# Three hand-written instruction orders of a retention and soft-MoE attention kernel are replaced

## The chip, the core and the metric

The kernel runs on one core of one Trainium2 chip. The metric is the device time of one execution in microseconds (us), less is better; the time of a version is the median of its runs. The engines of a core are TensorE (PE in the profile, with its weight loads as PEld), VectorE (DVE), ScalarE (ACT), GpSimd (POOL) and SyncE (SP, which issues the transfers here).

## What is computed

Eight batches of 576 tokens pass through two layers. The first is retention with eight heads of 64, the second a mixture of four attention experts of which each token takes the two best.

```python
scores = scale * np.matmul(q, k.transpose(0, 1, 3, 2))     # per head
ret = scores * Dmat            # gamma_h ** (i - j) for i >= j, else 0
x = np.matmul(ret, v)          # heads side by side: B x 576 x 512
logits = x @ w_gate            # the two best of four experts, softmax over them
for e in range(E):
    q, k, v = x @ wq[e], x @ wk[e], x @ wv[e]
    a = softmax(causal(scale * (q @ k.transpose(0, 2, 1))))
    ye = a @ v @ wo[e]
    out += weight_of_e * ye
```

## The kernel before, in words

The tokens are cut into 36 tiles of 128 rows (two chunks of 64; in four tiles the chunks come from two batches), and three tiles make a group, so there are 12 groups. Work runs as a pipeline over groups: in step j the retention of the tiles 3j+1 to 3j+3 is made, group j-1 gets its value, key and query projections and its gate, group j-2 its expert attention, and group j-3 its output projection. One unit of expert attention is one tile of one group, except that each third group ends in two half units ("tails"), so that three kinds of steps repeat. With t the number of earlier 128-blocks that a unit looks back on, a step works on units of t = 0, 1, 2 (kind A, j = 2, 5, 8, 11), t = 3, 0, 1 (kind B, j = 3, 6, 9) or t = 2, 3 and two tails of t = 4 (kind C, j = 4, 7, 10).

The order of all instructions on PE, DVE, ACT and POOL is written out by hand in three lists of tokens: `HEAD` (fills the pipeline), `STEP` (played for j = 2 to 11) and `TAIL` (drains it). `play` walks a list and calls one helper for each token; each engine then runs its instructions in that order and waits in that order. SP is not in the set `ORDERED`, so the order of its transfers is not given by the lists.

The tokens that matter here, with the line of the helper's instruction:

- Retention, argument is the tile: `qm` scores (PE, L197), `qa` their copy (ACT, L204), `qp` the causal cut (POOL, L210); `tm`/`tv` state products (PE, L170) and sums (DVE, L183, L185); `om`/`oa` product with the old state (PE, L223) and copy (ACT, L232); `wm`/`wv` product within the chunk (PE, L243) and sum (DVE, L252, L253); `dc` decay of the loaded values (POOL, or DVE with `:v`, L157); `sc` scaling (L261, L263), `xh`/`xl` the rounded part (ACT, L275) and the rest (L280).
- Projections: `vm` values and gate logits (PE, L335), `va` (ACT, L344, L349) and `vv` (DVE, L357, L358) their copies; `km`/`ka`, `hm`/`ha` keys and queries (PE, L316; ACT, L323, L325); `g.0` to `g.4` the gate (DVE, part 1 on ACT, L370 to L391). `wh`/`wl` split a weight into a rounded part and a rest (ACT, L298; DVE, L303), `tb` makes a decay table (ACT, L150).
- Units, first digit the unit, second the expert or block group: `s` scores (PE, L419; tails L427), `r` row limits (DVE, L443; tails L446), `e` powers (ACT, L456), `n` the factors (DVE, L464 to L466), `ma`/`mv` the scaling of one expert's powers on ACT (L480) or DVE (L482), `tt` transposes of up to four blocks into one bank (PE, L498), `ca`/`cv` their copy on ACT (L509) or DVE (L511), `ym` product with the values (PE, L532 to L539), `ya`, `yp`, `yl` its copy and split (ACT, POOL; DVE in the end).
- `pm`/`pa` output projection (PE, L565) and its copy with the store (ACT, L570).

All products land in PSUM, in one pool of eight banks. A product takes the bank that, by the plan made when the kernel is built, has come free first, and waits until that bank's last reader is done. Banks are requested where the products stand in the lists, so the lists also set which copy frees whose bank. A scores token of t = 0 or 1 takes two banks, one of t = 2, 3 or a tail four, `qm`, `om`, `wm`, `tm` two, the others one.

```python
pool = ctx.enter_context(tc.tile_pool(name="ps", bufs=8, space=bass.MemoryType.PSUM))
ctx.enter_context(tc.manual_schedule(engines=ORDERED))
```

Of the kernel before, what the change touches and what calls it, by code (L numbers as in the profile page):

```python
# [66 lines left out]
TAIL = """
@12 s.0 r.00 r.01 r.02 r.03 km.0 ka.0 e.00 e.01 e.02 e.03 n.0 ma.00 mv.01 ma.02 mv.03 hm.0 ha.0 s.1 r.10 r.11 r.12
r.13 km.1 ka.1 e.10 e.11 e.12 e.13 n.1 ma.10 mv.11 ma.12 mv.13 hm.1 ha.1 s.2 r.20 r.21 r.22 r.23 vm.0 va.0 vv.0 e.20
e.21 e.22 e.23 n.2 ma.20 mv.21 ma.22 mv.23 vm.1 va.1 vv.1 vm.2 va.2 vv.2 @13 s.0 r.00 r.01 r.02 r.03 @12 g.0 g.1 g.2  # L70
g.3 g.4 pm.0 pa.0 pm.1 pa.1 tt.00 cv.00 tt.01 ca.01 tt.02 cv.02 tt.03 ca.03 tt.10 ca.10 tt.11 cv.11 tt.12 ca.12
tt.13 cv.13 tt.20 cv.20 tt.21 ca.21 tt.22 cv.22 tt.23 ca.23 @13 s.1 r.10 r.11 r.12 r.13 e.00 e.01 e.02 e.03 n.0
ma.00 mv.01 ma.02 mv.03 @12 pm.2 pa.2 pm.3 pa.3 ym.0 ya.0 yp.0 ym.1 ya.1 yp.1 ym.2 ya.2 yp.2 @13 tt.00 cv.00 tt.01
ca.01 tt.02 cv.02 tt.03 ca.03 e.10 e.11 e.12 e.13 n.1 ma.10 mv.11 ma.12 mv.13 s.2 r.20 r.21 r.22 r.23 s.3 r.30 r.31
r.32 r.33 e.20 e.21 e.22 e.23 n.2 ma.20 mv.21 ma.22 mv.23 pm.0 pa.0 pm.1 pa.1 e.30 e.31 e.32 e.33 n.3 ma.30 mv.31
ma.32 mv.33 pm.2 pa.2 pm.3 pa.3 tt.10 ca.10 tt.11 cv.11 tt.12 ca.12 tt.13 cv.13 tt.20 cv.20 tt.21 ca.21 tt.22 cv.22
tt.23 ca.23 tt.30 ca.30 tt.31 cv.31 tt.32 ca.32 tt.33 cv.33 ym.0 yl.0 ym.1 yl.1 ym.2 yl.2 ym.3 yl.3 @14 pm.0 pa.0
pm.1 pa.1 pm.2 pa.2 pm.3 pa.3
"""


# [606 lines left out]
```

## Time and profile before

| | us |
|---|---|
| median of 3 runs | 471.57 (471.18 to 471.76) |
| the profiled execution | 473.03 |
| its span, first to last instruction | 470.9 |
| PE busy | 439.0 (93%) |
| ACT busy | 284.9 (61%) |
| DVE busy | 275.6 (59%) |
| POOL busy | 202.9 (43%) |

The profiled execution is 2.1 us longer than its span and 1.5 us above the median. The profile was read in this order: busy shares of the engines, busy time by stage, what PE waited for, the timeline of every engine around those waits, the chain of work that ended last, and the granted clock of TensorE in each stage.

### The profile page before, as it was taken

How to read it: one execution, taken by the hardware profiler on the slowest of the kernel's cores; microseconds unless marked ns; L12 is line 12 of the kernel's file. 1: busy time of each engine (PE TensorE's matmuls, PEld its weight loads, DVE VectorE, ACT ScalarE, POOL GpSimd, SP SyncE). 2: the span in 40 equal slices, each digit the busy share in tenths (PEclk: the TensorE clock that was granted, in tenths of full speed). 3: DMA queues.
4: the chain of work that ended last, by engine and by line, in shares of the span. 5: the costliest groups of instructions: out<-in, count | busy, mean ns of one | idle time of the engine just before them, and what ended most of it. 6: DMA issues, size and time to landing. Idle time of an engine off the chain costs nothing.

```text
span 470.9 us, 18834 instructions
## 1 busy us (share of the span) xinstructions
PE 439.0 (93%) x7916; PEld 397.5 (84%) x7916; DVE 275.6 (59%) x1083; ACT 284.9 (61%) x830; POOL 202.9 (43%) x260
## 2 busy tenths in 40 slices
...
PEclk9679878999999999999999999999999999999989
...
GB/s 273 407 118 100 221 124 101 56 162 125 84 135 124 1 145 197 21 151 169 53 165 125 1 128 212 7 151 185 41 173 84 1 22 51 3 1 35 35 68 68
DMA packets 18899, 50.90 MB, mean 108 GB/s; under 512 B 2304, under 2 KB 9088, under 8 KB 18816
## 3 DMA queue, kind: packets, MB, share of 16 engines
...
q8 instruction: 63, 1.03, 0.9%
q14 instruction: 20, 0.16, 0.1%
...
## 4 chain that ended last, share of the span: by engine, by line
PE 76%; ACT 9%; DVE 8%; issue 4%; DMA 1%; POOL 1%; SPq 0%; ACTq 0%; DVEq 0%; POOLq 0%
PE pj L316 22%; PE pv L335 11%; PE pt L498 7%; PE ss L419 6%; PE ys L532 6%; PE po L565 5%; PE own L243 5%; PE st L170 4%; PE qk L197 3%; PE old L223 3%; ACT p L456 2%; PE ys L539 2%; ACT p L480 2%; DVE sm L464 2%; PE ys L536 2%
## 5 line engine op out<-in xcount | busy, mean ns | idle before, releaser
L456 ACT ACTIVATE p<-p,nm 128x128 f32<-128x128 f32 (+8 forms) x144 | 79.8, 562 | 7.7 <-DVE nm L443 6.8
L280 POOL TENSOR_TENSOR xl<-x,xh 128x512 fp32r<-128x512 f32 x32 | 40.9, 1278 | 97.0 <-ACT xh L275 97.0
L443 DVE CUSTOM_DVE_ANT_0 p<-ss,mask 128x128 f32<-128x128 f32 (+7 forms) x128 | 51.0, 454 | 35.5 <-PE ss L419 35.5
L210 POOL TENSOR_SCALAR_AFFINE_SELECT p<-p 64x512 f32<-64x512 f32 x72 | 49.2, 683 | 33.1 <-ACT p L204 30.3
L480 ACT ACTIVATE p<-p,sm 128x64 f32<-128x64 f32 (+4 forms) x72 | 37.0, 556 | 38.5 <-DVE sm L466 38.5
L511 DVE COPY pth<-pt 128x512 f32<-128x512 f32 (+2 forms) x56 | 33.0, 612 | 43.6 <-PE pt L498 42.9
L555 POOL CAST yh<-y 128x256 fp32r<-128x256 f32 (+1 forms) x36 | 13.7, 382 | 80.9 <-ACT y L543 80.9
L419 PE MATMUL ss<-k,q 64*64 64x512 f32 (+7 forms) x512 | 42.2, 414 | 3.5 <-ACT ot L570 3.5
L263 POOL TENSOR_TENSOR x<-x,gi 128x512 f32<-128x512 f32 x26 | 33.6, 1290 | 21.8 <-DVE x L253 19.6
L498 PE MATMUL pt<-con,p 128*128 128x128 f32 x360 | 41.7, 273 | 0.5 <-ACT ot L570 0.5
L498 PEld LDWEIGHTS pt<-con,p 128*128 128x128 f32 x360 | 40.0, 141 | 1.2 <-ACT ot L570 0.7
L532 PE MATMUL ys<-pth,vn 128*64 128x128 f32 (+1 forms) x640 | 39.2, 254 | 0.0
L243 PEld LDWEIGHTS own<-p,vk 64*64 64x64 f32 x1152 | 28.1, 144 | 10.8 <-issue 8.9
L464 DVE TENSOR_SCALAR sm<-sm 128x4 f32<-128x4 f32 (+1 forms) x40 | 14.4, 361 | 34.8 <-ACT p L456 34.3
L157 POOL TENSOR_TENSOR vk<-vk,con 128x512 f32<-128x512 f32 x33 | 34.5, 1045 | 0.3
L243 PE MATMUL own<-p,vk 64*64 64x64 f32 x1152 | 30.9, 230 | 2.9 <-issue 2.6
L170 PE MATMUL st<-vk 64*64 64x64 f32 x1024 | 25.1, 230 | 8.3 <-issue 6.3
L204 ACT ACTIVATE p<-qk 128x256 f32<-128x256 f32 x72 | 23.5, 381 | 13.3 <-PE qk L197 12.8
L509 ACT ACTIVATE pth<-pt 128x512 f32<-128x512 f32 (+2 forms) x48 | 24.7, 548 | 10.1 <-PE pt L498 10.1
L532 PEld LDWEIGHTS ys<-pth,vn 128*64 128x64 f32 x640 | 29.0, 138 | 1.4 <-issue 0.9
L482 DVE TENSOR_SCALAR p<-p,sm 128x64 f32<-128x64 f32 (+4 forms) x104 | 29.1, 333 | 1.4
L253 DVE TENSOR_TENSOR x<-x,own 128x256 f32<-128x256 f32 (+1 forms) x72 | 25.5, 386 | 7.5 <-ACT x L232 6.6
...
## 6 DMA issues: line engine op xcount, KB each, us to landing
...
rg<-wraw SPq DMA_DIRECT2D x1, 8.0 KB, 7.9
```

The lines of the kernel that those rows point to most:

```text
L170: mm(ps[r][HALF[g], s, u], vk[HALF[r], s, 1, h], vk[HALF[r], s, 0, h], start=True, stop=True)
L210: gp.affine_select(w, w, pattern=[[0, 8], [1, 64]], base=0, channel_multiplier=-1, compare_op=OP.is_ge, fill=0.0)
L243: mm(ps[r][HALF[u], g, i], vk[HALF[r], s, 0, 2 * g + u], p[HALF[r], g, s, u], start=True, stop=True)
L280: e.tensor_sub(xl, x32, f(xh))
L316: mm(ps, ww[:, kc, p * 128:(p + 1) * 128], xx[:, kc], start=(i == 0), stop=(i == 11))
L335: mm(ps, xx[:, kc, l0:l0 + 128], ww[:, kc], start=(i == 0), stop=(i == 11))
L419: mm(ps[e][HALF[p]], q[p][HALF[z], l0 + 64 * s:l0 + 64 * s + 64], k[p][HALF[z], kb:kb + ws[e]], start=True, stop=True)
L443: v.tensor_tensor_reduce(p32[:, e, :ws[e]], ps[e], mask[:, 576 - ws[e]:], -1.0, BIG, OP.add, OP.min, nm[:, e:e + 1])
L456: act(p32[:, e, :ws[e]], p32[:, e, :ws[e]], AF.Exp, bias=nm[:, b:b + 1], scale=-1.0, accum_out=sm[:, 0, e:e + 1])
L480: act(o, i, AF.Copy, scale=rs[:, e:e + 1])
L498: nc.tensor.transpose(pt[:, z], src, ident)
L532: mm(py[HALF[z], p], VN[n0 + j][:, e * D:(e + 1) * D], src, start=(j == 0), stop=False)
```

## The change

Only the three lists are rewritten; no helper, tile or buffer is touched. Each list holds as many tokens as before. In `STEP` the order on PE stays mostly as it was up to `km.0`, with these moves: `om.0` comes before `qm.1`, `s.1` before `om.1`, `pm.3` before `pm.2`, and the transposes of the first units stand between `hm.0`, `hm.1` and `km.1` instead of behind all four. On ACT the copies `va`, `pa`, `qa`, `oa` stand ahead of scalings; on DVE `n.0` stands ahead of `vv.0`; on POOL `dc.2` opens the step, and `dc.3` stands ahead of `qp.2`. Of each step's scalings two go from ACT to DVE net, and of its transposed blocks' copies one more is on DVE. In `HEAD` three multiplies and subtractions move to DVE and three to POOL (`dc.1`, `sc.4`, `sc.5` to POOL; `dc.6`, `dc.7`, `xl.1` to DVE), the weight splits move forward or back in their queues, and `hm.0` goes behind `vm.2`. In `TAIL` the units of the last two groups, which alternated in blocks, are mixed token by token.

```diff
 STEP = """
-qm.1 qa.1 qp.1 om.0 oa.0 s.0 r.00 r.01 r.02 r.03 wm.0 wv.0 tm.1 tv.1 lx.3 lk.4 sc.0 dc.2 e.00 e.01 e.02 vm.0 va.0
-vv.0 e.03 n.0 ma.00 mv.01 ma.02 mv.03 xh.0 xl.0 vm.1 va.1 vv.1 pm.0 pa.0 pm.1 pa.1 qm.2 qa.2 qp.2 om.1 oa.1 s.1 r.10
-r.11 r.12 r.13 wm.1 wv.1 tm.2 tv.2 lx.4 lk.5 sc.1 dc.3 e.10 e.11 e.12 vm.2 va.2 vv.2 e.13 n.1 ma.10 mv.11 ma.12
-mv.13 xh.1 xl.1 pm.2 pa.2 pm.3 pa.3 qm.3 qa.3 qp.3 om.2 oa.2 s.2 r.20 r.21 r.22 r.23 wm.2 wv.2 tm.3 tv.3 s.3 r.30
...
+dc.2 om.0 qm.1 qa.1 qp.1 s.0 r.00 r.01 oa.0 r.02 r.03 wm.0 wv.0 tm.1 tv.1 sc.0 e.00 e.01 e.02 vm.0 va.0 e.03 n.0
+vv.0 ma.02 xh.0 mv.00 xl.0 mv.01 mv.03 lx.3 vm.1 va.1 vv.1 pm.0 pa.0 pm.1 pa.1 qm.2 dc.3 s.1 r.10 lk.4 om.1 qa.2
+oa.1 r.11 tm.2 r.12 e.11 r.13 wm.1 tv.2 qp.2 vm.2 e.10 e.12 lx.4 wv.1 lk.5 e.13 qm.3 n.1 mv.11 pm.3 pa.3 qa.3 pm.2
+e.32 va.2 om.2 oa.2 vv.2 pa.2 sc.1 mv.12 ma.10 xh.1 xl.1 qp.3 s.2 r.21 r.32 r.20 wm.2 wv.2 tm.3 e.21 r.22 r.23 e.20
+tv.3 s.3 km.0 e.22 e.23 sc.2 r.31 mv.33 r.30 r.33 hm.0 n.2 mv.21 tt.03 ka.0 tt.01 mv.32 e.30 mv.20 ma.13 e.31 n.3
+ma.31 dc.4 ma.30 hm.1 tt.00 ma.23 xh.2 mv.22 ca.23 xl.2 cv.00 ha.1 tt.02 lk.6 tt.10 tt.11 km.1 cv.10 cv.03 ha.0 ka.1
+cv.01 lx.5 cv.02 cv.11 tt.12 tt.20 e.33 ca.20 tt.21 tt.30 ca.12 tt.13 cv.13 tt.22 ca.22 tt.32 ca.21 g.0 cv.30 tt.31
+ym.0 ca.32 ya.0 yp.0 ym.1 tt.23 ca.31 g.1 ya.1 cv.33 yp.1 ym.2 ya.2 ym.3 g.2 tt.33 ya.3 yp.2 yp.3 g.3 g.4
 """
```

Of `HEAD`, the stretches that the prediction speaks of:

```diff
-qp.2 dc.2:v wh.v om.1 oa.1 wm.1 wv.1 tb.2 tm.2 tv.2 wl.v sc.1:v xh.1 xl.1 @1 vm.0 va.0 vv.0 @0 wh.k om.2 oa.2 wm.2
-wv.2 wl.k sc.2:v lx.4 lk.4 qm.3 qa.3 qp.3 @1 vm.1 va.1 vv.1 @0 xh.2 xl.2:v wh.q dc.3 @1 km.0 ka.0 @0 wl.q tm.3 tv.3
...
-@0 xh.4 xl.4:v lx.7 lk.8 @1 g.0 g.1 g.2 g.3 g.4 @0 qm.6 qa.6 qp.6 tb.4 om.5 oa.5 wm.5 wv.5 tm.6 tv.6 dc.7 sc.5:v
+qp.2 dc.2:v tv.1 om.1 oa.1 tm.2 xl.0 wl.v lk.4 wv.1 tb.2 sc.1:v xh.1 xl.1:v tv.2 @1 vm.0 va.0 @0 wh.k om.2 oa.2 wm.2
+@1 vv.0 @0 wv.2 lx.4 @1 vm.1 va.1 @0 sc.2:v qm.3 dc.3 lk.5 qa.3 wl.k qm.4 qp.3 xh.2 xl.2:v @1 vv.1 @0 wh.q fw.o @1
...
+va.2 @0 sc.4 @1 vv.2 hm.0 @0 xh.4 @1 g.0 g.1 @0 qm.6 @1 g.2 @0 xl.4:v lk.8 @1 g.3 @0 lx.7 qa.6 om.5 @1 g.4 @0 oa.5
+qp.6 lk.7 wm.5 wv.5 dc.7:v wh.o @1 ha.0 @0 tm.6 tv.6 sc.5 xh.5 wl.o xl.5:v lk.9 lx.8
```

Of `TAIL`, the stretch with the two tails (`s.2`, `s.3` of group 11):

```diff
-ca.01 tt.02 cv.02 tt.03 ca.03 e.10 e.11 e.12 e.13 n.1 ma.10 mv.11 ma.12 mv.13 s.2 r.20 r.21 r.22 r.23 s.3 r.30 r.31
-r.32 r.33 e.20 e.21 e.22 e.23 n.2 ma.20 mv.21 ma.22 mv.23 pm.0 pa.0 pm.1 pa.1 e.30 e.31 e.32 e.33 n.3 ma.30 mv.31
...
+@13 n.1 ma.10 ma.22 ma.11 s.3 r.30 s.2 r.20 ma.12 r.21 r.31 r.32 e.20 e.21 r.33 pm.2 pa.2 e.22 e.23 n.2 pm.1 mv.13
+e.30 pa.1 mv.20 mv.21 e.31 ma.23 pm.0 pa.0 tt.11 ma.32 tt.10 e.33 n.3 ma.31 mv.30 pm.3 tt.33 pa.3 tt.13 tt.12 cv.10
```

## Rows read from the trace of the kernel before

**Rows 1.** The page: busy time of PE and PEld over the span with their shares and instructions (only this one line), and TensorE's granted clock in 40 equal slices, in tenths of 2.4 GHz.

```profile
PE 439.0 (93%) x7916; PEld 397.5 (84%) x7916; DVE 275.6 (59%) x1083; ACT 284.9 (61%) x830; POOL 202.9 (43%) x260
...
PEclk9679878999999999999999999999999999999989
```

**Rows 2.** Busy time of each engine by stretch: the head up to the first projections of `STEP`, the last stretch, then one step of kind B (j = 6), of kind C (j = 7) and of kind A (j = 8). After the busy times of PE, PEld, DVE, ACT and POOL come the granted clock, the DMA share and GB/s.

```profile
0.00:74.61 74.61, 58.21 (x1373) 49.81 (x1373) 40.62 (x134) 35.73 (x108) 32.93 (x53) 0.82 0.59 205
...
395.34:470.90 75.56, 67.44 (x710) 59.84 (x710) 39.67 (x158) 43.62 (x121) 9.11 (x14) 0.98 0.10 36
...
197.50:231.18 33.68, 32.88 (x634) 30.46 (x637) 20.99 (x90) 21.92 (x67) 17.37 (x21) 1.00 0.35 119
231.18:272.33 41.15, 40.19 (x740) 36.13 (x742) 26.70 (x101) 26.42 (x70) 19.88 (x26) 1.00 0.30 98
272.33:304.05 31.72, 31.15 (x606) 29.22 (x608) 17.80 (x75) 20.43 (x65) 16.88 (x21) 1.00 0.36 127
```

**Rows 3.** The chain that ended last, in order of time (start, length, what), in the steps j = 5 and 6: what PE needs for its products when nothing is late. `pj` are four projections, `po` two output projections.

```profile
183.81 8.54 PE pj L316 x48
192.35 2.29 PE pt L498 x21
...
209.64 1.63 PE pv L335 x12
211.26 2.11 PE po L565 x12
213.38 0.62 PE qk L197 x32
214.00 0.47 PE old L223 x32
```

**Rows 4.** Timelines of four engines (start, length, engine, instruction, idle time before and what ended it) around PE's wait in a step of kind B: PE's scores `s.1`, ACT's scaling `ma.00` and `ma.02`, DVE's first instruction of `n.0`, POOL's `dc.2`.

```profile
208.02 0.55 PE L419 MATMUL ss<-k,q 64*64 64x64 f32 x13 [0.75 <-ACT ot L570]
...
205.36 1.28 ACT L480 ACTIVATE p<-p,sm 128x448 f32<-128x448 f32 x2 [1.55 <-DVE sm L466]
...
203.85 1.01 DVE L464 TENSOR_SCALAR sm<-sm 128x4 f32<-128x4 f32 x1 [0.20 <-ACT p L456]
...
203.79 1.04 POOL L157 TENSOR_TENSOR vk<-vk,con 128x512 f32<-128x512 f32 x1
```

**Rows 5.** PE's timeline: `s.2` in the middle and the start of `s.3` in a step of kind C, then `s.2` in the middle in one of kind A.

```profile
250.26 0.72 PE L427 MATMUL ss<-k,q 64*64 64x64 f32 x8 [0.88 <-ACT ot L570]
...
252.26 1.15 PE L427 MATMUL ss<-k,q 64*64 64x512 f32 x14
...
288.18 0.93 PE L419 MATMUL ss<-k,q 64*64 64x384 f32 x5 [0.57 <-ACT ot L570]
```

**Rows 6.** Timelines of ACT and DVE in the step j = 6: `va.1` (two copies), `pa.0` and `pa.1`, `qa.2` (two copies) on ACT, and `vv.1` (two copies) on DVE.

```profile
207.07 0.36 ACT L344 ACTIVATE vn<-pv 128x256 f32<-128x256 f32 x1
207.34 0.26 ACT L349 ACTIVATE vd<-pv 64x128 f32<-64x128 f32 x1
207.50 0.85 ACT L570 ACTIVATE ot<-po 128x384 f32<-128x384 f32 x2
208.24 0.64 ACT L204 ACTIVATE p<-qk 128x256 f32<-128x256 f32 x2
...
207.63 0.28 DVE L357 COPY vd<-pv 64x128 f32<-64x128 f32 x1 [1.35 <-ACT vd L349]
207.93 0.16 DVE L358 COPY lg<-pv 128x4 f32<-128x4 f32 x1
```

**Rows 7.** The head: PE's timeline at four waits, then DVE's at `tv.2` (L185), `sc.2` (L263) and `g.4` (L391), then the busy times and the clock (third number from the end) of the stretch from 55 to 64 us.

```profile
21.91 0.49 PE L170 MATMUL st<-vk 64*64 64x64 f32 x8 [2.98 <-issue]
...
24.60 1.23 PE L335 MATMUL pv<-wlv,xh 128*128 128x260 f32 x4 [1.03 <-DVE wlv L303]
...
32.66 0.97 PE L316 MATMUL pj<-xh,whk 128*128 128x384 f32 x4 [1.15 <-ACT xh L275]
...
55.07 0.71 PE L223 MATMUL old<-x,s 64*64 64x64 f32 x16 [1.82 <-DVE s L185]
...
22.44 0.89 DVE L185 TENSOR_TENSOR s<-st,s 128x128 f32<-128x128 f32 x4 [2.63 <-PE st L170]
...
30.64 1.14 DVE L263 TENSOR_TENSOR x<-x,gi 128x512 f32<-128x512 f32 x1
...
52.26 1.77 DVE L391 TENSOR_TENSOR wt<-ex,mx 64x6 f32<-64x6 f32 x4
...
55.00:64.00 9.00, 7.95 (x116) 7.67 (x117) 6.11 (x26) 4.75 (x16) 4.09 (x4) 0.50 0.38 118
```

**Rows 8.** SP's timeline: the load of the last weight, whose token `fw.o` stands in the middle of `HEAD`.

```profile
13.32 0.33 SPq L287 DMA_DIRECT2D raw<-wraw  x1
```

**Rows 9.** The tail: PE's `pm.0` of group 10 and a later transpose, DVE's `n.1` and the limits `r.20`, `r.21` of the first tail unit, and the busy times and the clock of the stretch in which PE makes four output projections.

```profile
446.90 0.98 PE L565 MATMUL po<-yh,who 128*128 128x384 f32 x2 [3.95 <-DVE nm L446]
...
455.85 1.31 PE L498 MATMUL pt<-con,p 128*128 128x128 f32 x10 [0.50 <-ACT ot L570]
...
444.55 0.17 DVE L464 TENSOR_SCALAR sm<-sm 128x4 f32<-128x4 f32 x1 [3.11 <-ACT p L456]
...
446.06 0.69 DVE L446 CUSTOM_DVE_ANT_0 p<-ss,mask 128x512 f32<-128x512 f32 x1
447.11 0.69 DVE L446 CUSTOM_DVE_ANT_0 p<-ss,mask 128x512 f32<-128x512 f32 x1
...
446.90:452.68 5.78, 5.78 (x25) 5.74 (x26) 4.06 (x19) 3.51 (x8) 0.00 (x0) 0.72 0.00 0
```

More of the change, by code (lines that the diff above doesn't have):

```diff
@@ L46 @@
 HEAD = """
-dc.0:v qm.0 qa.0 qp.0 tm.0 tv.0 dc.1:v qm.1 qa.1 qp.1 om.0 oa.0 wm.0 wv.0 tb.1 sc.0:v tm.1 tv.1 xh.0 xl.0 qm.2 qa.2
-qp.2 dc.2:v wh.v om.1 oa.1 wm.1 wv.1 tb.2 tm.2 tv.2 wl.v sc.1:v xh.1 xl.1 @1 vm.0 va.0 vv.0 @0 wh.k om.2 oa.2 wm.2
-wv.2 wl.k sc.2:v lx.4 lk.4 qm.3 qa.3 qp.3 @1 vm.1 va.1 vv.1 @0 xh.2 xl.2:v wh.q dc.3 @1 km.0 ka.0 @0 wl.q tm.3 tv.3
-lx.5 lk.5 fw.o lk.6 qm.4 qa.4 qp.4 @1 km.1 ka.1 @0 dc.4 tb.3 om.3 oa.3 wm.3 wv.3 tm.4 tv.4 dc.5 sc.3:v @1 hm.0 ha.0
-@0 qm.5 qa.5 qp.5 xh.3 xl.3:v lx.6 lk.7 @1 hm.1 ha.1 @0 om.4 oa.4 wm.4 wv.4 tm.5 tv.5 dc.6 sc.4:v @1 vm.2 va.2 vv.2
@@ L52 @@
-@0 xh.4 xl.4:v lx.7 lk.8 @1 g.0 g.1 g.2 g.3 g.4 @0 qm.6 qa.6 qp.6 tb.4 om.5 oa.5 wm.5 wv.5 tm.6 tv.6 dc.7 sc.5:v
-xh.5 xl.5:v lx.8 lk.9 wh.o wl.o
+dc.0:v qm.0 qa.0 qp.0 tm.0 tv.0 dc.1 qm.1 qa.1 qp.1 tb.1 om.0 oa.0 wm.0 wv.0 qm.2 sc.0:v tm.1 wh.v xh.0 wm.1 qa.2
+qp.2 dc.2:v tv.1 om.1 oa.1 tm.2 xl.0 wl.v lk.4 wv.1 tb.2 sc.1:v xh.1 xl.1:v tv.2 @1 vm.0 va.0 @0 wh.k om.2 oa.2 wm.2
+@1 vv.0 @0 wv.2 lx.4 @1 vm.1 va.1 @0 sc.2:v qm.3 dc.3 lk.5 qa.3 wl.k qm.4 qp.3 xh.2 xl.2:v @1 vv.1 @0 wh.q fw.o @1
+km.0 ka.0 @0 tm.3 qa.4 @1 km.1 @0 lx.5 @1 ka.1 @0 tv.3 wl.q qp.4 om.3 oa.3 wm.3 lk.6 dc.4 tb.3 wv.3 dc.5 sc.3:v qm.5
@@ L54 @@
+qa.5 qp.5 xh.3 tm.4 @1 hm.1 @0 tv.4 om.4 oa.4 wm.4 xl.3:v tb.4 @1 ha.1 @0 lx.6 tm.5 @1 vm.2 @0 wv.4 dc.6:v tv.5 @1
+va.2 @0 sc.4 @1 vv.2 hm.0 @0 xh.4 @1 g.0 g.1 @0 qm.6 @1 g.2 @0 xl.4:v lk.8 @1 g.3 @0 lx.7 qa.6 om.5 @1 g.4 @0 oa.5
+qp.6 lk.7 wm.5 wv.5 dc.7:v wh.o @1 ha.0 @0 tm.6 tv.6 sc.5 xh.5 wl.o xl.5:v lk.9 lx.8
 """
 STEP = """
-qm.1 qa.1 qp.1 om.0 oa.0 s.0 r.00 r.01 r.02 r.03 wm.0 wv.0 tm.1 tv.1 lx.3 lk.4 sc.0 dc.2 e.00 e.01 e.02 vm.0 va.0
-vv.0 e.03 n.0 ma.00 mv.01 ma.02 mv.03 xh.0 xl.0 vm.1 va.1 vv.1 pm.0 pa.0 pm.1 pa.1 qm.2 qa.2 qp.2 om.1 oa.1 s.1 r.10
```

22 lines of the change are left out of this document (9 added, 13 removed).

## The prediction

> **What bounds the kernel now.** The busy shares come first: PE is busy for 439.0 of 470.9 us, and every other engine has more than a third of the span free [rows 1]. So a new order can give back only what PE loses by waiting, 31.9 us at most, and what it loses at the lower clock. The busy times by stage say where that is [rows 2]: the head leaves 74.61 - 58.21 = 16.4 us idle at a mean clock of 0.82, the last stretch 8.1 us, and a step between only 0.80 us (kind B), 0.96 (C) or 0.57 (A). A step is PE's own work, so steps can't shrink much, though there are ten. The chain that ended last gives what each product costs PE without a wait: 2.13 us for a projection (8.54 over four), 1.63 for a value tile, 1.05 for an output projection, 0.62 and 0.47 for `qm` and `om`, 0.11 for a transposed block (2.29 over 21) [rows 3]. These spacings, and not the modelled busy share, are used below.
>
> **Steps: what goes.** In kind B, PE stands 0.75 us in front of `s.1` for a bank that `pa` frees. ACT comes late to `pa`, since it first waits 1.55 us for `n.0` and then makes two scalings in 1.28; `n.0` took 1.01 us for a four-column multiply because it ended only with POOL's `dc.2` (203.79 + 1.04 = 204.83) [rows 4]. The new list takes three things from this line: `dc.2` opens the step, `n.0` stands ahead of `vv.0`, and `ma.00` becomes `mv.00`. And `s.1` comes one product earlier, so that two banks fewer are taken when it asks. In C and A half of `s.2` waits for `pa.2` and `pa.3`, which stand on ACT behind the scalings: 0.88 and 0.57 us [rows 5]. In C there is 0.7 more: between 250.26 and 252.26 PE has a last quarter of `s.2` (0.2), `wm.2` (0.6) and `tm.3` (0.5), 1.3 us of work in 2.0, because banks come one by one. So there go 0.80 (B), 0.96 + 0.70 = 1.66 (C), and 0.57 in two steps of kind A (the first runs in the head's disturbance, and the last makes no new tiles): 3 x 0.80 + 3 x 1.66 + 2 x 0.57 = 8.5.
>
> **Steps: what is late next.** `pa.3` and `qa.3` now stand on ACT straight behind `pm.3`: a lag of 0.2, then 0.38 and 0.53 [rows 6], 1.1 us, which `pm.2` and `om.2` cover with 1.05 + 0.47 = 1.52 [rows 3]. So `s.2` has its banks, as long as the plan doesn't hand it `vm.2`'s, whose copies `va.2` (0.54) and `vv.2` (0.3 to 0.5) come behind these [rows 6]: with that bank the wait would be 2.1 - 1.5 = 0.6 us. `om.1` needs `va.1` and `pa.0`; adding up ACT's line I find these 0.4 to 0.8 us ahead of PE. The transposes that move between the projections I cost at nothing: `tt.0x` have had their scalings since the first third of the step, `tt.1x` need `ma.13`, which ACT reaches some 2 us before PE gets there, and their copies lie beside `km.1` (2.13). Without that cover the price is what is left of one copy, under 0.6. Two more scalings and one more copy on DVE, 0.3 to 0.6 us each, lie beside some 13 us in which DVE idles in such a step [rows 2]. I leave 0.3 in each of the eight steps for what I haven't seen: -8.5 + 2.4 = **-6.1 us**. Bounds: -8.5, and +0.5 with 0.6 in front of `s.2` in each step and 0.3 to 0.4 elsewhere.
>
> **Transfers.** SP's order isn't the list's: the load whose token `fw.o` stands in mid-head was issued at 13.32 us [rows 8]. So where loads and stores go is open. I take nothing for it; a load has most of a step to land.
>
> **Head.** DVE reached `wl.v` only after `tv.2`, which waited 2.63 us for a product that PE made late (an "issue" gap of 2.98), and so the first value tile stood 1.03 us for its low weights [rows 7]. Now `wl.v` stands ahead of `wv.1` and `tv.2`; the gaps named issue should stay, since as many instructions stand ahead of them. -1.0. `wl.k` goes behind `sc.2`, which it held up, so `xh.2`, for which the first projection waited 1.15, comes up to that much earlier [rows 7]; I take -0.7, since `vm.1` and its copies now stand ahead of `xh.2`. Then the gate: DVE works through `g.0` to `g.4` until 54 us, and `tv.6`, which PE's `om.6` needs, stands behind it (1.82 us of idle shown, and the clock at 0.50 from 55 to 64 [rows 7]). In the new list the gate still stands ahead of `tv.6`, with `dc.7` added on DVE (0.7), but `hm.0` (2.13) lies beside it as work for PE. -0.8. Sum **-2.5 us**. Bounds: +1, if `dc.7` in DVE's queue waits for its load and holds `tv.6`; -6, if PE no longer falls to the lower level of 1.2 GHz (7.95 us of work at half speed are 4.0 too many).
>
> **Tail.** PE stands 3.95 us in front of `pm.0`, for a bank that `r.20` frees. DVE makes `r.20` only after `n.1`, for which it idles 3.11 us until ACT has made the four powers of the unit before [rows 9]. After the gap the four output projections take 5.78 us at a mean clock of 0.72, where 4 x 1.05 = 4.22 would do: 1.56 lost. The new list spreads those powers among the copies of group 10 and puts `ym.1` and three transposes in front of the tails, so that `n.1` is over about when `s.3` is. Then DVE makes `r.30` (1.05 with both halves) and the first half of `r.20` (0.69) [rows 9], 1.7 us, while PE has `s.2` (1.1), `pm.2` and `pm.1` (2.1): `pm.0` finds a bank. 3.95 + 1.56 + 0.50 (in front of a late transpose) = 6.0; I leave 0.5, for the scaling `ma.31` that stands on ACT behind four copies and that `tt.31` needs: **-5.5 us**. Bounds: -6.3, and -2.5, if a wait of 2 us stays and the clock falls again.
>
> **Sum.** -6.1 - 2.5 - 5.5 = -14.1. The profiled execution would go from 473.0 to 458.9, its span from 470.9 to 456.8; against the median of the runs, 471.57 - 14.1 = **457.5 us**.
>
> **Rivals.** (1) DVE and POOL hold each other up. The row is the `n.0` of 1.01 us that ended with POOL's instruction, against 0.17 in the tail where POOL was idle [rows 4, 9]. If `n.0` meets a POOL instruction again (`sc.0` should end 0.3 to 1 us ahead of it), it is late by up to 1.2, of which some 0.65 is beyond the margin of `om.1`: 10 x 0.65 = +6.5, 464.0 us. The Trainium skill has this as a rule that speaks against the change (SBUF — State Buffer, "SBUF: two separate sides"): the port pair that VectorE shares with GpSimd is locked for a whole instruction, and the other engine blocks. By that rule each scaling and multiply that goes to DVE may wait out a POOL instruction, and the sum would be this rival's. Chance 0.16. (2) All waits go: -8.5 - 6 - 6.3 = -20.8, 450.8 us. Against it: DVE's gate still stands ahead of `tv.6`. Chance 0.09. (3) The copies gain nothing by their places, since each waits for its own product, and PE's waits merely move: 471.6 us. For it speaks that PE idles under 1 us in each step. Chance 0.05. (4) Slower: `s.2` is handed `vm.2`'s bank, and `vv.2`, which stands on DVE behind `n.1` and `mv.11`, is held by one POOL multiply of 1.3 us: a wait of 0.6 + 1.3 = 1.9 us in all ten steps, +19 - 3 (the rest left above), 473.5 us. After a wait of 1.8 us in the head the clock stood at 0.50 [rows 7], and the tail's gap cost 1.56 that way [rows 9]; with this in each step it would be 489. It decides from a mean wait of 1.7 us per step. Against it: `n.1` should be over 2 us before `va.2`. Chance 0.10.
>
> **How the numbers follow.** The forecast with its smaller errors (452 to 463) has 0.58; 0.02 is left for two of the mishaps at once. A difference of 0.2% (0.9 us) is about what measuring this kernel can tell from none. Faster: 0.58 + 0.16 + 0.09 + 0.02 = 0.85; same 0.05; slower 0.10. The range reaches to the second rival and beyond the first: 450.0 to 468.0.
>
> **What would show it.** Right: no wait of PE on an ACT `ot` in front of scores in the steps; the DVE instruction L464 near 0.2 us at `n.0`; steps of kind C 1 to 1.6 us shorter, of kind B 0.5 to 0.8; PE's wait in front of the late output projections gone and the clock there at 1.0; the first value tile without a wait on `wlv`. Wrong: a new wait in front of `s.2` that ends with a copy from `pv` (L349, L357, L358), waits of PE on `pt` copies, steps longer than before, or an idle PE of 2 us and more in the tail.

## The result and the profile after

| | before | after |
|---|---|---|
| median, us | 471.38 (471.06 to 471.76, 4 runs) | 445.13 (444.68 to 445.50, 4 runs) |
| span of the profiled execution, us | 470.9 | 443.1 |

The ratio is 0.9442, 95% interval 0.9426 to 0.9459: 26.2 us less, where 14.1 were forecast. The time lies below the range. Of the runs further down, one execution of e11 took 978.72 us, more than twice any other; e11's median holds it, and its ratio leaves it out.

The page after: PE's and PEld's busy time, and the granted clock in 40 slices.

```profile
PE 427.4 (96%) x7916; PEld 387.3 (87%) x7916; DVE 302.4 (68%) x1095; ACT 275.9 (62%) x818; POOL 205.3 (46%) x260
...
PEclk9779899999999999999999999999999999999999
```

PE idles 15.7 us instead of 31.9 [rows 1], and its busy time itself fell by 11.6: the same 7916 instructions, fewer of them at the lower clock (mean granted clock 0.964 before, 0.985 after) or strung out while banks came one by one. The 11.6 were not split between the two. The prediction's bound named idle time and the lower clock, but not work strung out.

Busy times by stretch, as in [rows 2]: the head up to the first projections of `STEP`, from there to the first projections of the last step, the rest, then the steps of kind B, C and A that answer to the three there.

```profile
0.00:65.64 65.64, 53.85 (x1373) 46.15 (x1373) 40.99 (x130) 35.08 (x105) 34.04 (x52) 0.90 0.64 230
65.64:373.77 308.13, 308.05 (x5838) 282.90 (x5835) 222.56 (x810) 195.45 (x589) 160.82 (x194) 1.00 0.32 107
373.77:443.10 69.33, 65.50 (x715) 58.27 (x710) 38.89 (x156) 45.40 (x127) 10.44 (x15) 1.00 0.11 39
183.63:216.37 32.74, 32.74 (x649) 30.36 (x645) 24.99 (x90) 19.85 (x63) 17.55 (x21) 1.00 0.37 123
216.37:255.80 39.43, 39.43 (x749) 35.35 (x744) 29.09 (x104) 25.42 (x70) 19.59 (x26) 1.00 0.31 103
255.80:286.64 30.84, 30.84 (x591) 28.89 (x585) 20.69 (x78) 20.33 (x64) 17.08 (x21) 1.00 0.38 130
```

Against [rows 2]: the head 74.61 - 65.64 = 9.0 shorter, the steps 395.34 - 74.61 - 308.13 = 12.6, the rest 75.56 - 69.33 = 6.2. Through the steps PE idles 0.08 us in all; a cycle of three steps takes 103.01 instead of 106.55.

What PE still waited for in the first 95 us (us in total, times, longest):

```profile
PE st L170 <- issue: 3.4, 1, 3.4
PE qk L197 <- DMA x<-xf: 3.1, 1, 3.1
PE old L223 <- DVE s L185: 2.1, 1, 2.1
...
PE pj L316 <- ACT xh L275: 0.8, 1, 0.8
```

The two largest are a gap named issue and the load of a tile, which PE now reaches before it has landed.

PE's timeline after at the places of [rows 7] and of [rows 9]:

```profile
23.06 1.07 PE L335 MATMUL pv<-wlv,xh 128*128 128x260 f32 x4
...
30.80 0.98 PE L316 MATMUL pj<-xh,whk 128*128 128x384 f32 x4 [0.80 <-ACT xh L275]
...
50.22 0.54 PE L223 MATMUL old<-x,s 64*64 64x64 f32 x16 [2.12 <-DVE s L185]
...
64.56 0.62 PE L243 MATMUL own<-p,vk 64*64 64x64 f32 x26 [0.43 <-DVE lg L358]
...
420.89 0.61 PE L565 MATMUL po<-yh,who 128*128 128x384 f32 x2
```

The wait on `wlv` is gone, that on `xh` 0.35 shorter, the one in front of the late output projections gone. The one behind the gate is even longer (2.12 for 1.82), but PE is past it 4.9 us earlier, and the clock behind it recovers sooner. The busy time of PE and the clock (third number from the end) after:

```profile
52.00:54.00 2.00, 2.00 (x48) 0.50 0.68 229
54.00:56.00 2.00, 2.00 (x15) 0.76 0.85 272
56.00:64.00 8.00, 7.78 (x219) 1.00 0.39 136
```

Before, the clock stood at 0.50 from 55 to 64 us [rows 7]: 1.2 GHz for at least 9 us against some 3.

### The profile page after: what moved, and what is told of

It is laid out like the page before. It is cut to its first block, busy times and chain, and to the rows that moved or that the text cites. A ratio compares the mean times of both kernels' runs of the same rounds, so it can differ in the third digit from the quotient of the medians.

```text
span 443.1 us, 18830 instructions
## 1 busy us (share of the span) xinstructions
PE 427.4 (96%) x7916; PEld 387.3 (87%) x7916; DVE 302.4 (68%) x1095; ACT 275.9 (62%) x818; POOL 205.3 (46%) x260
## 4 chain that ended last, share of the span: by engine, by line
PE 86%; issue 3%; ACT 2%; DVE 2%; POOL 2%; DMA 2%; SPq 1%; DVEq 0%; POOLq 0%; ACTq 0%
PE pj L316 22%; PE pv L335 11%; PE po L565 11%; PE pt L498 8%; PE ss L419 7%; PE ys L532 7%; PE qk L197 4%; PE own L243 3%; PE old L223 3%; PE st L170 3%; PE ys L539 2%; DMA vk<-vkf 2%; PE ss L427 2%; PE ys L536 2%; POOL p L210 1%
## 5 line engine op out<-in xcount | busy, mean ns | idle before, releaser
L443 DVE CUSTOM_DVE_ANT_0 p<-ss,mask 128x320 f32<-128x320 f32 (+7 forms) x128 | 51.6, 454 | 16.3 <-PE ss L419 16.1
L482 DVE TENSOR_SCALAR p<-p,sm 128x64 f32<-128x64 f32 (+8 forms) x116 | 46.2, 448 | 0.9
L498 PE MATMUL pt<-con,p 128*128 128x128 f32 x360 | 44.4, 273 | 0.1
L263 POOL TENSOR_TENSOR x<-x,gi 128x512 f32<-128x512 f32 x28 | 36.6, 1307 | 16.1 <-DVE x L253 12.5
L480 ACT ACTIVATE p<-p,sm 128x512 f32<-128x512 f32 (+7 forms) x60 | 31.3, 547 | 14.9 <-DVE sm L466 14.7
L419 PE MATMUL ss<-k,q 64*64 64x512 f32 (+7 forms) x512 | 37.0, 405 | 0.0
L570 ACT ACTIVATE ot<-po 128x384 f32<-128x384 f32 x48 | 22.4, 486 | 19.0 <-PE po L565 18.8
L323 ACT ACTIVATE k<-pj 128x384 f32<-128x384 f32 x24 | 11.8, 491 | 33.7 <-PE pj L316 33.5
L243 PEld LDWEIGHTS own<-p,vk 64*64 64x64 f32 x1152 | 24.7, 141 | 5.1 <-issue 4.5
L232 ACT ACTIVATE x<-old 128x256 f32<-128x256 f32 (+1 forms) x72 | 22.0, 361 | 11.4 <-PE old L223 11.0
```

The lines of the kernel that those rows point to most:

```text
L243: mm(ps[r][HALF[u], g, i], vk[HALF[r], s, 0, 2 * g + u], p[HALF[r], g, s, u], start=True, stop=True)
L419: mm(ps[e][HALF[p]], q[p][HALF[z], l0 + 64 * s:l0 + 64 * s + 64], k[p][HALF[z], kb:kb + ws[e]], start=True, stop=True)
L443: v.tensor_tensor_reduce(p32[:, e, :ws[e]], ps[e], mask[:, 576 - ws[e]:], -1.0, BIG, OP.add, OP.min, nm[:, e:e + 1])
L482: v.tensor_scalar(o, i, rs[:, e:e + 1], None, op0=OP.mult)
L498: nc.tensor.transpose(pt[:, z], src, ident)
```

## Do the three lists add up?

The theory: the gain is the sum of three separate parts, and the head's and the steps' are larger than forecast. The rival: the parts depend on each other. The edit of each run is one list of the new kernel in the kernel before (e1 to e3), or the old `HEAD` in the new kernel (e4).

```diff
# e1: HEAD new, STEP and TAIL old     # e2: STEP new     # e3: TAIL new
# e4: HEAD old, STEP and TAIL new
```

> Only HEAD is the new list; STEP and TAIL are the old ones. Theory 1 (the gain is the sum of three separate parts, and the head's is about 10 us because PE no longer works at the lower clock behind the gate and because the 1.97 us gap named issue in front of the first step's wm.2 was a wait for a bank): 461 to 462 us, and the landmarks of the new kernel up to the first projections of STEP at about 65 to 67 us. Theory 2 (the head's part was forecast rightly at 2.5 us, and the rest of what is seen there comes from the new STEP, whose first play overlaps the head's end): 467 to 469 us.

> Only STEP is new. Theory 1 (additive; steps give 11 to 12 us, as the per-step waits and the slow stretches around them go): 459 to 461 us, steps of kind B, C, A at about 32.7, 39.4 and 30.9 us. Theory 2 (the first step's gap and lower clock go with STEP too): 453 to 457 us. The forecast's own term would be 465.

> Only TAIL is new. The forecast's term stands (5.5 us): 465 to 467 us with the wait of 3.95 us in front of the late output projections gone. Rival: the old STEP's last play leaves banks and engines later, so that the new TAIL's order meets waits: 468 to 470 us.

> The new kernel with the old HEAD. If the parts add up: 445 + 10 = 455 us. If the head's gain needs the old STEP's copies, or the new STEP alone takes away the first step's gap, less: 448 to 452 us.

| run | us | kernel before beside it | ratio, 95% interval |
|---|---|---|---|
| e1 head | 464.12 | 471.52 | 0.9849 [0.9819, 0.9879] |
| e2 steps | 458.42 | 471.52 | 0.9731 [0.9705, 0.9757] |
| e3 tail | 465.58 | 471.52 | 0.9888 [0.9868, 0.9908] |
| e4 new, old head | 453.05 | 471.52 | 0.9618 [0.9591, 0.9646] |

7.4 + 13.1 + 5.9 = 26.4: the parts add up to the whole, and e4 gives the head 453.05 - 445.13 = 7.9. Both my sizes for the first theory were off: the head is 7.4 and not 10, the steps 13.1 and not 11 to 12. The first theory gave the head a gap that is not its own, in front of `wm.2` of the first step, which the profile names issue. In e1 it is still there (PE's timeline):

```profile
65.30 0.94 PE L243 MATMUL own<-p,vk 64*64 64x64 f32 x30 [1.90 <-issue]
...
66.70 1.27 PE L316 MATMUL pj<-xh,whk 128*128 128x384 f32 x4
```

Its clock by stretch:

```profile
56.00:66.00 10.00, 6.83 (x213) 1.00 0.51 160
66.00:70.00 4.00, 4.00 (x62) 0.64 0.40 133
```

So the gap comes with the old `STEP`, not with `HEAD`. In e2 PE waits only 0.64 us at that product; in e4, which has the same `HEAD` and `STEP` as e2, it waits 0.64 there and 1.08 more, again named issue, one product further on. The four slow microseconds behind the gap do not come with it every time, as the last section shows. What the gap waits for can be read in the kernel before, in a stretch that I had not read closely:

```profile
71.41 0.85 ACT L480 ACTIVATE p<-p,sm 128x192 f32<-128x192 f32 x2 [1.44 <-DVE sm L466]
72.17 0.61 ACT L275 ACTIVATE xh<-x 128x512 fp32r<-128x512 f32 x1
72.68 0.63 ACT L204 ACTIVATE p<-qk 128x256 f32<-128x256 f32 x2
73.15 0.94 PE L243 MATMUL own<-p,vk 64*64 64x64 f32 x30 [1.97 <-issue]
```

PE goes on 0.47 us after the copy `qa.3` begins, which stood behind two scalings and a rounding. That fits a wait for a bank, of the kind that I priced in later steps, under another name; e5 below tests it.

## The steps: copies, factors, transposes

e5 moves only copies ahead of scalings in the old `STEP`; e6 makes the edit that the prediction priced for kind B, without moving `s.1`; e7 takes the transposes back out of the projections in the new `STEP`; e10 puts them there in the old one.

```diff
 e5, STEP before
-n.1 ma.10 mv.11 ma.12 mv.13 xh.1 xl.1 pm.2 pa.2 pm.3 pa.3 qm.3 qa.3 qp.3
+n.1 mv.11 mv.13 pm.2 pa.2 pm.3 pa.3 qm.3 qa.3 ma.10 ma.12 xh.1 xl.1 qp.3
 e6, STEP before
-qm.1 qa.1 ... sc.0 dc.2 e.00 ... va.0 vv.0 e.03 n.0 ma.00 mv.01
+dc.2 qm.1 qa.1 ... sc.0 e.00 ... va.0 e.03 n.0 vv.0 mv.00 mv.01
 e7, STEP after
-hm.0 n.2 mv.21 tt.03 ka.0 tt.01 ... hm.1 tt.00 ma.23 xh.2 mv.22 ca.23 xl.2 cv.00 ha.1 tt.02 lk.6 tt.10 tt.11 km.1
+hm.0 n.2 mv.21 ka.0 ... hm.1 ma.23 xh.2 mv.22 xl.2 ha.1 lk.6 km.1 tt.03 tt.01 tt.00 ca.23 cv.00 tt.02 tt.10 tt.11
 e10, STEP before
-km.1 ka.1 hm.1 ha.1 tt.00 cv.00 ... tt.11 cv.11
+km.1 ka.1 tt.00 cv.00 ... tt.11 cv.11 hm.1 ha.1
```

> The kernel before, with one stretch of STEP changed: pa.2, pa.3 and qa.3 stand ahead of ma.10, ma.12 and xh.1 (ACT), nothing else. Theory 1 (the steps' gain is banks that come free earlier because copies no longer stand behind scalings; this also takes the first step's gap of 1.97 us in front of wm.2 and the stretch at the lower clock behind it, 1.75 us): 3 x 1.66 + 2 x 0.57 + 3.7 = 9.8 less, 461 to 463 us. Theory 2 (the copies gain nothing by their places alone; STEP's gain comes from the transposes among the projections and the moves to DVE): 469 to 472 us. If only the steps' part is right and the first step's gap is something else: 465 to 466 us.

> The kernel before, with STEP's first third changed: dc.2 opens the step on POOL, n.0 stands ahead of vv.0 on DVE, and ma.00 becomes mv.00. Forecast's term (the line of ACT in front of pa.0 and pa.1 gets shorter, the wait of 0.75 us in front of s.1 goes in three steps of kind B): 2.4 us less, 468.5 to 469.5 us. Rival (s.1 only waits for the next bank, or DVE's added scaling delays the steps): 471 to 473 us.

> The new kernel, with STEP's transposes of the first units and their copies put back behind all four projections. Forecast (the place of the transposes is worth nothing, a copy's remainder at most): 445 to 446 us. Rival (transposes among the projections keep PE from waiting on their copies, some 0.8 us in each step): 450 to 454 us with waits of PE on pt copies.

> The kernel before, with hm.1 and ha.1 in STEP put behind the transposes tt.00 to tt.11 and their copies, so that these stand among the projections as in the new list. Forecast (worth nothing by itself): 470.5 to 472 us. Rival (it is a gain of its own, of the size that e7 lost, about 1.5 us in each step of kind B): 466 to 468 us.

| run | us | kernel before beside it | ratio, 95% interval |
|---|---|---|---|
| e5 | 465.06 | 471.53 | 0.9856 [0.9827, 0.9884] |
| e6 | 467.06 | 471.53 | 0.9894 [0.9869, 0.9920] |
| e7 | 450.09 | 471.53 | 0.9545 [0.9522, 0.9567] |
| e10 | 471.83 | 471.51 | 1.0010 [0.9988, 1.0032] |

e5 gives 6.5, short of the 9.8 expected, and clear of the rival. The waits of PE in e5 from 95 to 400 us:

```profile
PE st L170 <- issue: 2.7, 5, 0.8
PE ss L419 <- ACT ot L570: 2.3, 3, 0.8
```

The second line is the three waits of kind B, which e5 does not touch. Those of kind C and A in front of `s.2` are gone, but five smaller ones stand in their place, in front of `tm.3`, and the profile names them issue. In the first step the gap has gone from `wm.2` to `tm.3` as well. PE's and ACT's timeline there:

```profile
71.36 0.91 PE L170 MATMUL st<-vk 64*64 64x64 f32 x32 [1.65 <-issue]
...
70.38 0.61 ACT L275 ACTIVATE xh<-x 128x512 fp32r<-128x512 f32 x1
70.90 0.64 ACT L232 ACTIVATE x<-old 128x256 f32<-128x256 f32 x2
```

PE goes on 0.46 us after the copy `oa.2` begins, and `oa.2` is the copy that e5 left behind the scalings and the rounding; the same pair stands in kind C (`oa.2` at 138.33, `tm.3` at 138.81). So these gaps are of the same sort as the ones that e5 took away, and e5 moved part of the loss to the next copy. Its time lies where its expectation put the case that the first step's gap is something else (465 to 466), but the trace gives this other reason. The clock no longer fell behind the first step's gap.

e6 gives 4.5 where the prediction had 2.4. From the first projections of the step j = 5 to those of j = 6, a stretch with the wait of 0.75 [rows 4] in it, it takes 213.19 - 181.61 = 31.58 instead of 216.54 - 183.74 = 32.80: 1.2 for 0.75. PE's idle time did not hold the whole loss there; its scores came in pieces around the wait, and count as busy. e5 and e6 give 11.0 of e2's 13.1; the rest was not split. Among it are two moves on PE that the list of moves ahead of the prediction leaves out: `qm.3` now stands ahead of `pm.3` and `pm.2`, and `tm.2` ahead of `wm.1`.

e7 loses 5.0, e10 gains nothing. The waits of PE in e7 from 95 to 400 us have, beside three gaps of 0.3 to 0.4 named issue, one new line, once in each step of kind B:

```profile
PE ys L532 <- DVE pth L511: 3.1, 3, 1.0
```

Around it, from the first projections of j = 3 to those of j = 4, e7 takes 134.24 - 97.61 = 36.63, the new kernel 132.42 - 97.32 = 35.10: 1.5 for each such step, 4.6 of the 5.0. So the place of the transposes is no gain by itself; it covers copies that the rest of the new list makes late. The prediction costed it at nothing with its cover, which held, and at under 0.6 without, which was too little. Why the old list, with its transposes last, has no such wait was not tried; that its copies had an emptier DVE (in a step of kind B 90 instructions in 20.99 us [rows 2], as many in 24.99 after) is only argued.

## The head: the early weight, the work beside the gate

e13 and e9 each make one of the prediction's head steps in the kernel before, e14 both; e15 takes `hm.0` away from the gate in the new kernel; e8 and e12 try to mend the wait of 2.12 us that is left.

```diff
 e13, HEAD before
-wv.1 tb.2 tm.2 tv.2 wl.v sc.1:v
+wl.v wv.1 tb.2 tm.2 tv.2 sc.1:v
 e9, HEAD before (e14: e9 and e13)
-sc.3:v @1 hm.0 ha.0 @0 qm.5 ... vm.2 va.2 vv.2 @0 xh.4 ... @1 g.0 g.1 g.2 g.3 g.4
+sc.3:v qm.5 ... vm.2 va.2 vv.2 hm.0 @0 xh.4 ... @1 g.0 g.1 ha.0 g.2 g.3 g.4
 e15, HEAD after
-tm.4 @1 hm.1 @0 ... vv.2 hm.0 @0 xh.4 ... wh.o @1 ha.0 @0 tm.6
+tm.4 @1 hm.0 ha.0 hm.1 @0 ... vv.2 @0 xh.4 ... wh.o tm.6
 e8, HEAD after (e12: also wh.o behind qa.4 and wl.o behind wl.q)
-@1 g.3 @0 lx.7 qa.6 om.5 @1 g.4 @0 oa.5 ... tm.6 tv.6 sc.5
+lx.7 qa.6 om.5 oa.5 ... tm.6 tv.6 @1 g.3 g.4 @0 sc.5
```

> The kernel before, with wl.v in HEAD ahead of wv.1, tb.2, tm.2 and tv.2. Forecast's step: the wait of 1.03 us in front of the first value tile's low weights goes, 470 to 471 us. Theory 1 (the values also come earlier by the 0.7 us that DVE's queue had left, and the lower clock ends earlier): 468.5 to 470 us. Rival (a later wait takes it back, the first projection's for xh): 471 to 472 us.

> The kernel before, with one move in HEAD: hm.0 goes behind vm.2 and its copy ha.0 between g.1 and g.2, so that PE has 2.1 us of work while DVE computes the gate. The forecast's step (0.8 us, the clock falls all the same): 470 to 471 us. Theory 1 (the wait of 1.82 us goes, PE doesn't fall to 1.2 GHz at 55 us, and the 4.0 us that this stretch costs are kept): 465 to 467 us, with the granted clock at 1.0 from 54 to 64 us. Rival (DVE's late work then stalls the first step instead): 469 to 472 us with the clock at 1.0.

> The kernel before, with the moves of e9 (hm.0 behind vm.2) and e13 (wl.v early) together. If these two carry the head's gain: 464 to 465.5 us, as e1. If the rest of HEAD (weight splits, choice of engine, state products) carries a share of its own: 466.5 to 468.5 us, the sum of both.

> The new kernel, with hm.0 and ha.0 in HEAD put back ahead of hm.1. Theory 1 (hm.0 covers DVE's gate and tv.6; without it the wait of 2.12 us grows by hm.0's 2.1 us): 446.5 to 449 us with a wait of some 4 us in front of the second half of om.6. Forecast's size of this step (0.8 us): 445.5 to 446.3 us.

> The new kernel, with the gate's parts g.3 and g.4 of HEAD (DVE, 2.0 us) put behind tv.6. If the wait of 2.12 us in front of the second half of om.6 is DVE's work on the gate and the clock falls at 51.4 us because of it: the wait is under 0.5 us, the clock stays at 2.4 GHz there, and the time is 2 to 4 us less, 441 to 443 us. Rival (DVE is then late for the first step, since row limits and factors stand behind the moved parts): the wait moves into the first step and the time stays at 444 to 446 us.

> The new kernel with g.3 and g.4 of HEAD behind tv.6, as in e8, and with the weight split wh.o and wl.o (1.05 us on ACT, 1.5 on DVE) moved from the end of HEAD to the idle stretch behind wl.q, so that DVE reaches the first step's row limits earlier than in e8. If the first step stands for DVE's line: 442 to 444 us. Rival (other work is late there, and nothing of the wait that e8 took away comes back): 444.5 to 446 us.

| run | us | kernel before beside it | ratio, 95% interval |
|---|---|---|---|
| e13 | 470.12 | 471.35 | 0.9974 [0.9953, 0.9996] |
| e9 | 468.77 | 471.51 | 0.9937 [0.9910, 0.9963] |
| e14 | 466.42 | 471.35 | 0.9891 [0.9863, 0.9920] |
| e15 | 448.64 | 471.35 | 0.9513 [0.9483, 0.9543] |
| e8 | 445.49 | 471.53 | 0.9457 [0.9423, 0.9491] |
| e12 | 444.63 | 471.51 | 0.9433 [0.9405, 0.9461] |

e13 gives 1.2, the forecast's 1.0. e9 gives 2.7, where the forecast had 0.8 and my theory 4.5 to 6.5. Its wait behind the gate fell from 1.82 to 0.35; the clock still fell, for some seven microseconds. The move need not be the reason that this is shorter than in the profile before: in e17 below, with the old `HEAD`, the clock is down for seven as well. PE's timeline of e9:

```profile
51.77 0.54 PE L223 MATMUL old<-x,s 64*64 64x64 f32 x16 [0.35 <-DVE s L185]
...
69.57 0.94 PE L243 MATMUL own<-p,vk 64*64 64x64 f32 x30 [2.12 <-issue]
```

Its clock by stretch:

```profile
52.00:58.00 6.00, 4.79 (x104) 0.52 0.68 224
...
69.00:72.00 3.00, 2.43 (x70) 1.00 0.13 41
```

Both together (e14) give 4.9, two thirds of e1's 7.4; the other 2.5 lies in edits of `HEAD` that were not split. e15 confirms the cover in the new list, at 3.5 us (PE's timeline of e15):

```profile
52.22 0.70 PE L223 MATMUL old<-x,s 64*64 64x64 f32 x16 [3.55 <-DVE s L185]
```

The wait that is left comes in part from the new `STEP`, which begins with `om.0` and no longer with `qm.1`: with the new `HEAD` and the old `STEP` (e1) PE waits 0.34 us for the same sum (`tv.6`), with the old `HEAD` and the new `STEP` (e2) 4.1. The prediction counted nothing for this.

e8 came out as the rival in its expectation. PE's wait there fell to 1.11 only, the clock stayed at 2.4 GHz from 28 us on, and the time did not move: DVE came no sooner to the first step (its first row limit starts at 53.78, for 53.56 in the new kernel), and PE waits there for what follows on ACT (PE's timeline of e8, then its busy time and the clock):

```profile
48.72 0.54 PE L223 MATMUL old<-x,s 64*64 64x64 f32 x16 [1.11 <-DVE s L185]
...
57.75 0.33 PE L243 MATMUL own<-p,vk 64*64 64x64 f32 x4 [0.52 <-ACT p L480]
59.19 0.68 PE L243 MATMUL own<-p,vk 64*64 64x64 f32 x28 [1.11 <-ACT p L204]
...
28.00:58.00 30.00, 26.79 (x747) 1.00 0.47 162
```

e12 frees DVE there and reaches 444.63, no measurable difference from the new kernel. No version measurably faster than the new one was found.

One caution: with `HEAD` and `STEP` untouched, the first projections of `STEP` began at 73.94 (e3), 75.35 (e11), 74.49 (e16) and 72.23 us (e17). One profile of this head tells nothing below some 3 us; the medians carry the readings above, and e13 is at their edge.

## The tail: one wait for another

The prediction named DVE's `r.20` behind `n.1` as the releaser of the wait of 3.95 us [rows 9]. e11 puts the limits first, e16 also the copies `pa`, e17 instead makes the powers of the unit before the tails early.

```diff
 e11, TAIL before
-e.13 n.1 ma.10 mv.11 ma.12 mv.13 s.2 r.20 ... s.3 r.30 ... r.33 e.20
+e.13 s.2 r.20 ... s.3 r.30 ... r.33 n.1 ma.10 mv.11 ma.12 mv.13 e.20
 e16: e11, and pm.0 pa.0 pm.1 pa.1 ahead of n.1, pm.2 pa.2 pm.3 pa.3 ahead of n.3
 e17, TAIL before
-ma.02 mv.03 @12 pm.2 pa.2 ... ca.03 e.10 e.11 e.12 e.13 n.1 ma.10 mv.11 ma.12 mv.13 s.2
+ma.02 mv.03 e.10 e.11 e.12 e.13 n.1 ma.10 mv.11 ma.12 mv.13 @12 pm.2 pa.2 ... ca.03 s.2
```

> The kernel before, with one move in TAIL: the row limits of the two tails (r.20 to r.33, with s.2 and s.3 in front of them) stand ahead of n.1 and the scalings ma.1x, mv.1x of the unit before. If the late wait of 3.95 us is DVE's r.20 behind n.1, as the forecast says, it goes with the lower clock behind it: 466 to 468 us (3.95 + 1.56 less, and up to 2 back for scalings that are late). Rival (the bank comes free no earlier, since the limits wait for s.3): 470 to 472 us.

> The kernel before, with e11's move in TAIL, and with pm.0 pa.0 pm.1 pa.1 ahead of n.1 and its scalings and pm.2 pa.2 pm.3 pa.3 ahead of n.3. If e11 lost its gain to the copies pa, which stood on ACT behind scalings and powers: the two waits of 2.12 and 2.64 us go, 465.5 to 468 us. Rival (the scalings of the tails become late and PE waits for their transposes): 470 to 473 us.

> The kernel before, with one move in TAIL: the powers e.10 to e.13 of the unit before the two tails, with its factors n.1 and scalings ma.1x, mv.1x, stand behind mv.03, ahead of the output projections pm.2 and pm.3 of group 9 and of the values ym.0 to ym.2, and so before the tails' scores. If the tail's gain is that ACT has these powers behind it when the tails' scores are done: the first power of a tail starts some 3.5 us after the scores instead of 6.5, and the time is 465.5 to 467.5 us. Rival (pa, ya and the copies of transposes then stand behind the powers, and PE waits there instead): 470 to 473 us.

| run | us | kernel before beside it | ratio, 95% interval | last stretch, us |
|---|---|---|---|---|
| e11 | 473.89 | 471.51 | 1.0048 [1.0030, 1.0066] | 77.6 |
| e16 | 471.77 | 471.35 | 0.9996 [0.9973, 1.0018] | 75.3 |
| e17 | 470.45 | 471.56 | 0.9977 [0.9961, 0.9992] | 75.2 |

The last stretch runs from the first projections of the last step to the end, 75.56 before [rows 2] and 69.33 after. In each run the named wait goes, and another comes: in e11 two for banks that `pa` frees, in e16 two for ACT's scalings of the tails, with the output projections that could have filled them already done, and one of 0.80 for `pa`, in e17 one in front of the tails' scores (PE's timelines of e11, e16, e17; the lists are a line shorter in these files, so line numbers are one less):

```profile
451.13 1.09 PE L497 MATMUL pt<-con,p 128*128 128x128 f32 x8 [2.12 <-ACT ot L569]
...
454.87 2.40 PE L497 MATMUL pt<-con,p 128*128 128x128 f32 x10 [2.64 <-ACT ot L569]
```

```profile
450.81 1.09 PE L497 MATMUL pt<-con,p 128*128 128x128 f32 x8 [1.75 <-ACT p L479]
...
453.80 2.18 PE L497 MATMUL pt<-con,p 128*128 128x128 f32 x9 [0.77 <-ACT p L479]
```

```profile
439.31 3.82 PE L426 MATMUL ss<-k,q 64*64 64x512 f32 x32 [2.68 <-DVE pth L510]
```

In none of the three did the expected gain come; e16 and e17 lie in the ranges of their rivals. The releaser named by the trace was real, and none of the three sets of moves is worth the 5.9 us of e3. What sets the new list apart shows in the powers: the first power of a tail starts 422.14 - 418.78 = 3.4 us after the start of the scores, before 447.23 - 440.77 = 6.5. But that alone does not do it: in e17 it is 442.64 - 439.31 = 3.3, and there the scores themselves were held up. Which smallest set of moves does it stays open. The scores and the first power, before, after and the power in e17:

```profile
440.77 2.18 PE L427 MATMUL ss<-k,q 64*64 64x512 f32 x32
447.23 0.78 ACT L456 ACTIVATE p<-p,nm 128x576 f32<-128x576 f32 x1 [0.72 <-DVE nm L446]
...
418.78 2.18 PE L427 MATMUL ss<-k,q 64*64 64x512 f32 x32
422.14 0.78 ACT L456 ACTIVATE p<-p,nm 128x576 f32<-128x576 f32 x1 [0.18 <-DVE nm L446]
...
442.64 0.78 ACT L455 ACTIVATE p<-p,nm 128x576 f32<-128x576 f32 x1 [0.35 <-DVE nm L445]
```

## Why the prediction was wrong, by its own steps

**The sum, -14.1.** The direction was right, and that the steps give most; two of three sizes were not, and the head, put last, gives more than the tail.

| step of the prediction | forecast | measured |
|---|---|---|
| steps | -6.1 | -13.1 (e2) |
| head | -2.5 | -7.4 (e1), -7.9 (e4) |
| tail | -5.5 | -5.9 (e3) |

**The steps** failed most, in three places. First, "the first runs in the head's disturbance": I left the first step out. From the first projections of the step j = 3 to those of the last step e2 takes 381.47 - 104.61 = 276.86, where the kernel before takes 395.27 - 108.97 = 286.30: 9.4 less, for a forecast of 6.1. So some 3.7 of e2's 13.1 lie outside the steps that I priced. The trace of e2 has 2.9 of it in front of the first projections of `STEP` (71.64 for 74.54) and 1.5 in the step behind them. The gap named issue is a late copy of the same sort (e5), but how much of the 3.7 is this gap isn't shown, since one order alone scatters by 3.1 us at that place. Second, "I leave 0.3 in each of the eight steps": 2.4 kept back for waits that did not come. In the new kernel no wait of PE stands between 75 and 380 us. Third, idle time as the price: the three steps' waits of 0.80 + 1.66 + 0.57 = 3.03 gave 106.55 - 103.01 = 3.54, and kind B alone 1.2 for 0.80 (e6). The mechanism, banks that come free when copies don't stand behind scalings, was right and is shown by e5, by the waits that went and by those that came behind the copy left in its place; the transposes' place is worth nothing alone (e10) and 5.0 as cover (e7).

**The head** failed at "-0.8" for the gate and at taking the lower clock as lasting, with its end as a mere bound. The work beside the gate gave 2.7 (e9) and is worth 3.5 in the new list (e15). From `s.0` to the first projections, 55.55 to 74.54 before, e1 needs 50.03 to 66.70, 2.3 less, at full clock to 66 us. In the new kernel the full clock by itself gave no time back (e8). The term for `wl.v`, 1.0, was right (e13: 1.2); the wait on `xh`, at 0.7 in the sum, got 0.35 shorter. "The gaps named issue should stay" held for the one in front of the first value tile (2.98, then 3.38). Of the three that stood in front of `tm` products in the first 95 us (6.3 in all) it is the only one left, though the load of 3.1 now stands near the place of the first; and the gap at `wm.2` isn't of that sort. For the 2.5 of the head's 7.4 that e14 leaves, no cause is shown.

**The tail** was right in size, and its three terms did go: no wait stands in front of the late output projections or the late transposes, and the clock is at 1.00 there. But the explanation by a single releaser was too narrow, since in e11 that wait goes and the time does not.

**The rivals.** The first, DVE and POOL holding each other up, did come true, only not at a price. The multiply `n.0` of kind B is 0.17 us now, but another one meets POOL (DVE's and POOL's timeline after):

```profile
229.27 1.29 POOL L263 TENSOR_TENSOR x<-x,gi 128x512 f32<-128x512 f32 x1 [2.18 <-DVE x L253]
229.36 1.23 DVE L464 TENSOR_SCALAR sm<-sm 128x4 f32<-128x4 f32 x1 [0.27 <-ACT p L456]
```

DVE's scalings after as a group (busy us, mean ns):

```profile
L482 DVE TENSOR_SCALAR p<-p,sm 128x64 f32<-128x64 f32 (+8 forms) x116 | 46.2, 448 | 0.9
```

The mean scaling on DVE went from 333 to 448 ns, with other shapes in the mix too; of one shape, 128x384, from 418 to 552. The rule that the Trainium skill gives (SBUF — State Buffer, "SBUF: two separate sides"), that one engine of the pair blocks for the other's whole instruction, agrees with the 1.23 beside 1.29. That it would cost 6.5 us did not follow: through the steps PE idles 0.08 us in all. The second rival, "all waits go", was nearest at 450.8 and still 5.7 too high, for the reasons above. The third is refuted by e5 and e6, and of the fourth there is no trace, since PE has no wait in front of `s.2`.
